# Keys in eight tiles, an account of the vector engine in the planner, and a reordered prologue

## Chip, core and metric

The kernel runs on one core of one Trainium2 chip. The metric is the device time of one execution in microseconds (us); a kernel's time is the median of its runs.

## What is computed

Two independent halves over 2048 positions of width 512, written side by side. Half A is attention with 32 query heads of width 16 that share one head of keys and values. Half B is a short and a long causal convolution per channel, with a multiplicative gate before and behind the long one.

```python
def _A_ref(x, wq, wk, wv, wo):
    q = (x @ wq).reshape(B, S, H, Dh).transpose(0, 2, 1, 3)
    k = x @ wk
    v = x @ wv
    scores = jnp.einsum("bhqd,bkd->bhqk", q, k) * (Dh ** -0.5)
    p = _softmax(scores, axis=-1)
    o = jnp.einsum("bhqk,bkd->bhqd", p, v)
    return o.transpose(0, 2, 1, 3).reshape(B, S, H * Dh) @ wo

def _B_ref(q, k, v, shift_k, ssm_k, ssm_D):
    k_shift = sum of four shifted copies of k times shift_k
    kv = k_shift * v
    y = irfft(rfft(pad(kv)) * rfft(pad(ssm_k)))[:S] + kv * ssm_D
    return q * y

return jnp.concatenate([a, b], axis=-1)
```

## The kernel before

**Engines.** TensorE (PE) does the products, ScalarE (ACT) the exponentials of the softmax, VectorE (DVE) reads the products out of PSUM and does the arithmetic of half B, GpSimd (POOL) some casts and many DMA issues, SyncE (SP) the other DMAs. Each engine runs its queue in order. The order on each is the order in which the program emits instructions (`manual_schedule`).

**Attention.** The scores are computed transposed: keys on the partitions, 512 queries of two head halves on the free axis. The work is cut into 32 stacks (`NQ`), each of 16 tiles of 128 keys times two halves `a`; with a few of them taken out (below) that makes 1016 score tiles, numbered u in the code. For each u, `scores` (through `keys`, L1039) issues eight matmuls of `kst` (keys, f16, with rows for the low parts and for a bound) against `st` (queries of the stack) into one of two PSUM buffers of the pool `ps`; `exp` (L1056) makes `p` out of it on ACT; `pv` (L1080) multiplies `p` with `vx` (values and a row of ones) and accumulates in a pair of PSUM banks `acc`, from the pool `pf`, over a whole stack. At a stack's end DVE adds the two banks into `ao` (L1089, L1090) and a DMA sends it to `od`. The softmax's shift is a bound from norms, not the true maximum; a row of `st` carries it.

**The filler.** `pf` has two pairs. One is held by the accumulation of the stack, the other goes in turn to all other products: query projections, the Fourier products of half B (`halves`, L250), the output projection. These are Python generators ("threads"): `own`, `wo_heads`, `conv_pe`, `conv_short`, `rest_of_q`, `wo_part`, `conv_dve`, `spill`. A thread yields `(n, cost, NEW or CONT, ...)` for n units of products, `(0, cost)` for DVE work, or `(WAIT, x)` to be asked again 2x score slots later. After each score tile `_Fill.turn` gives a slot's spare PE time (`SLOT` = 916 ns less `SCORES` = 220 and `PV` = 430 for each accumulation) to the first thread that fits, and DVE work against a credit of `RATE` = 850 ns for each slot. A thread that is in the middle of its products holds the pair (`holder`, CONT); after its last product the next NEW one is let in `GAP` = 2 slots later. The planner does not know how far behind DVE is. `after(...)` lets a thread wait until another has emitted something.

**The early stretch.** The prologue transposes x, projects the first queries, finds the maximum of the absolute keys (`kv_max`, L630), from which `k_max` and `k_row` (L649 to L653) make a clipped maximum over all keys and `wbn` (L831) the row of bounds. `k_first` (L624) makes the first 512 keys, `k_cut` and `k_split` (L664, L671, L673) clip them and split them into `kst`. Two products with `sel` place the queries (L823, L827), one with `wbn` (L833) adds the bound, and `st` is copied from PSUM. The other three chunks of 512 keys are made in `rest_of_q` among the first 32 score tiles (`k_chunk`, `v_turn`), out of the tile `kvt`.

**`own`.** In the stacks `OWN_IN` (27 to 30) the last key tile is not exponentiated by ACT: `own` puts its scores into the fill pair (a = 0, then a = 1), DVE reads each twice (L1137, L1138) and computes the exponential as a polynomial (L1148), and the result is accumulated by `pv` when `attend` finds it in `owed`.

## Time and profile before

| what | us |
|---|---|
| median of 3 runs | 1009.33 |
| the three runs | 1011.52, 1009.33, 1003.33 |
| the profiled execution, whole | 1009.57 |
| its span, first to last instruction | 1007.7 |

The profile is of one execution. Its rows give the start and the busy time of groups of instructions, an engine and a line of the kernel, and what is written from what. A bracket `[0.98 <-POOL wkv L273]` gives the engine's idle time ahead of the group and the instruction that ended it. A row `x14` stands for 14 instructions that overlap or follow closely. Page 5's groups end in the busy time, the mean duration in ns, and the idle time just before. In the windows, each engine has its busy time and its number of instructions, then come the clock that PE was granted (1.00 is full), the share of the DMA engines and GB/s. The mean granted clock of the execution was 0.988.

### The profile page before, as it was taken

Reading aid. Unit: us, or ns where it says so; the run is one execution under the profiler, and the core shown is the slowest. Engines: PE = TensorE matmul, PEld = TensorE weight load, DVE = VectorE, ACT = ScalarE, POOL = GpSimd, SP = SyncE. Lnnn points to the kernel's source line nnn. Section 1 sums busy time; section 2 is a strip of 40 time slices with the busy share of each in tenths; the row PEclk is TensorE's granted clock in tenths of the full one; section 3 lists DMA queues with packets and bytes.
Section 4 is the critical chain, followed back from the end, with each engine's and each line's share of the span. In section 5 each row is a group of like instructions: output and inputs, shape, how many; then the busy total and the mean of one; then the engine's idle time right before and its main releaser. Section 6 shows DMA issues by size and latency. Waiting matters only on the chain.

```text
span 1007.7 us, 51389 instructions
## 1 busy us (share of the span) xinstructions
PE 945.7 (94%) x23517; PEld 460.7 (46%) x23517; DVE 751.1 (75%) x985; ACT 952.5 (95%) x1031; POOL 173.2 (17%) x320
## 2 busy tenths in 40 slices
PE   7899989989999999999999999999989999989996
PEld 4334544435454444444444445544434444444453
DVE  4555578789529989989898568789979947576853
ACT  4779999999999999999999999999999999999994
POOL 6031122321113000101433332000000122200000
PEclk9979999999999999999999999999999999999999
DMA  7242343332114212321343333110121232221101
GB/s 246 96 119 69 96 136 106 86 98 65 53 42 135 62 42 74 109 63 54 110 124 122 115 96 94 43 53 31 59 85 44 74 124 88 76 64 32 33 25 47
DMA packets 69207, 82.94 MB, mean 82 GB/s; under 512 B 20753, under 2 KB 58295, under 8 KB 68983
## 3 DMA queue, kind: packets, MB, share of 16 engines
q1 hardware_dynamic: 47558, 43.48, 13.6%
q0 software_dynamic: 20320, 35.46, 12.0%
q8 instruction: 186, 3.05, 1.3%
q10 hardware_dynamic: 1104, 0.64, 0.2%
q14 instruction: 39, 0.31, 0.1%
HBM read 54.46 MB, written 25.03 MB: 79 GB/s over the span
## 4 chain that ended last, share of the span: by engine, by line
PE 49%; ACT 30%; DVE 12%; issue 7%; POOL 1%; DMA 1%; ACTq 0%; DVEq 0%
ACT p L1056 30%; PE f L1080 24%; PE s L1039 14%; PE f L250 10%; DVE own L1148 2%; DVE sp L169 2%; DVE ao L1089 1%; DVE ao L1090 1%; DMA wkvf<-in_A_wk 1%; DVE sp L290 1%; DVE sp L435 0%; PE f L638 0%; DVE sp L219 0%; PE f L658 0%; DVE u L218 0%
## 5 line engine op out<-in xcount | busy, mean ns | idle before, releaser
L1056 ACT ACTIVATE p<-s 128x1024 f32<-128x1024 f32 x1012 | 935.7, 1068 | 28.9 <-PE s L1039 26.7
L1080 PE MATMUL f<-p,vx 64*32 64x512 f32 (+1 forms) x8848 | 551.0, 558 | 2.9 <-DVE sp L290 2.1
L1039 PE MATMUL s<-st,kst 49*32 49x512 f16 x8128 | 425.8, 383 | 34.6 <-ACT p L1056 26.9
L1039 PEld LDWEIGHTS <-kst 49*32 49x32 f16 x8192 | 197.5, 90 | 402.1 <-issue 350.5
L1080 PEld LDWEIGHTS f<-p,vx 64*32 64x32 f32 x8848 | 175.4, 107 | 32.6 <-issue 6.2
L169 DVE TENSOR_TENSOR sp<-sp 128x1024 f32<-128x1024 f32 x96 | 111.0, 1214 | 0.0
L290 DVE COPY sp<-f 128x1024 f32<-128x1024 f32 x32 | 39.1, 1223 | 68.0 <-PE f L250 68.0
L295 POOL DMA_DIRECT2D ff<-in_ff x64 | 35.2, 556 | 266.3 <-ACT p L1056 265.4
L250 PE MATMUL f<-wo,o 64*32 64x512 f16 x1440 | 56.9, 375 | 1.9 <-DVE r L468 1.6
L169 DVE TENSOR_TENSOR sp<-sp,sp 128x1024 f32<-128x1024 f32 x48 | 56.3, 1217 | 0.3
L250 PE MATMUL f<-xT,wq 64*32 64x512 f16 x1344 | 51.9, 375 | 0.0
L1089 DVE COPY ao<-f 128x512 f32<-128x512 f32 (+1 forms) x33 | 22.2, 674 | 36.8 <-PE f L1080 36.7
L295 POOL DMA_DIRECT2D fi<-in_fi x32 | 17.4, 547 | 181.2 <-ACT p L1056 180.4
L250 PE MATMUL f<-a,ff 64*32 64x256 f32 x1024 | 42.3, 382 | 3.4 <-DVE t L396 1.5
L250 PE MATMUL f<-sp,fi 64*32 64x256 f32 x1024 | 40.5, 376 | 2.0 <-DVE r L468 2.0
L250 PE MATMUL f<-hT,ff 64*32 64x256 f32 x1024 | 40.7, 377 | 0.7 <-DVE sp L290 0.4
L470 POOL DMA_DIRECT2D out<-r x32 | 17.3, 546 | 128.1 <-DVE r L468 128.1
L468 DVE TENSOR_TENSOR r<-f,q 128x512 f32<-128x512 f32 x16 | 11.0, 690 | 31.9 <-PE f L250 31.8
L405 DVE TENSOR_TENSOR a<-a,t 128x512 f32<-128x512 f32 x48 | 33.2, 691 | 1.5
L396 DVE TENSOR_TENSOR t<-kk,tpb 128x512 f32<-128x512 f32 (+1 forms) x50 | 33.0, 663 | 0.0
L323 POOL DMA_DIRECT2D hin<-in_B_ssm_k x32 | 21.1, 663 | 58.6 <-ACT p L1056 57.1
L250 PEld LDWEIGHTS <-o 64*32 64x32 f16 x1440 | 22.4, 93 | 17.0 <-issue 3.2
(191 smaller groups left out, 747.3 us busy)
## 6 DMA issues: line engine op xcount, KB each, us to landing
ff<-in_ff POOLq DMA_DIRECT2D x64, 128.0 KB, 2.6
od<-ao SPq DMA_DIRECT2D x60, 128.0 KB
qd<-qp SPq DMA_DIRECT2D x48, 128.0 KB
st<-qd SPq DMA_DIRECT2D x62, 98.0 KB
kk<-in_B_k POOLq DMA_DIRECT2D x32, 128.0 KB, 2.4
v<-in_B_v POOLq DMA_DIRECT2D x32, 128.0 KB, 3.0
hin<-in_B_ssm_k POOLq DMA_DIRECT2D x32, 128.0 KB, 5.8
fi<-in_fi POOLq DMA_DIRECT2D x32, 128.0 KB, 3.3
```

What stands on the lines that cost most here:

```text
L169: v.tensor_tensor(part(out), part(a), part(b), op)
L250: y = self.nc.tensor.matmul(out[j : j + 32, cols], w[r, j : j + 32], x[r], start=half == m == 0, stop=half == 1 and m == k - 1,)
L290: self.nc.vector.tensor_copy(out, self.both.rearrange("p i (q n) -> p i q n", q=2))
L295: self.paced(self.nc.gpsimd.dma_start(t[:, i], self.I[n][:, 2 * m2 + i]))
L323: self.paced(nc.gpsimd.dma_start(dst, src))
L396: nc.vector.tensor_tensor(out[:, n], kk[:, x], tap(i, n.stop - n.start), ALU.mult)
L405: nc.vector.tensor_tensor(a, a, t, ALU.add)
L1039: self.nc.tensor.matmul(s[j : j + 32, e, :], self.kst[rows, k * P + j : k * P + j + 32], self.st[n][rows, a, cols], start=True, stop=True,)
L1056: self.exps[u % 4] = self.nc.scalar.activation(self.pt[u], s, AF.Exp, scale=LN2 * DH**-0.5 / SC / SC)
L1080: nc.tensor.matmul(self.acc[e][32 * j : 32 * j + 32, m], vx[rows, :], y, start=k == 0, stop=stop)
L1089: nc.vector.tensor_copy(a, self.acc[0][:, m])
L1148: v.scalar_tensor_tensor(g, g if i < 4 else y, c[i], y if i else x.bitcast(BF16), ALU.add, ALU.mult)
```

## The change

**Account of DVE.** The emitter keeps `now` (the score slot), `dve` (the planner's time at which DVE will have done all that has been given to it) and `ready` (such times for the pairs, one appended whenever a holder gives up a pair or an accumulation ends, one removed whenever a pair is taken). `charge` adds a cost, `due` asks if a time has come, `mark` records when a named result will be there.

```diff
     def pair(self):
+        del self.ready[:1]
         return self.pf.tile([P, 2, 512], F32, tag="f", name=self.nm("f"))
+    def charge(self, cost, pe):
+        self.dve = max(self.dve, SLOT * self.now + 700 * pe) + cost
+    def due(self, t):
+        return SLOT * self.now + 300 >= t
+    def mark(self, x):
+        self.seen.add(x)
+        self.when[x] = self.dve
     def after(self, *what):
-        while not self.seen.issuperset(what):
-            yield WAIT, 1
+        while not all(x in self.seen and self.due(self.when.get(x, 0)) for x in what):
+            yield WAIT, 0.5
...
-                    if n < 1 or self.holder not in (None, t) or (self.holder is None and i < self.free):
+                    if n < 1 or self.holder not in (None, t):
+                        continue
+                    if self.holder is None and (i < self.free or not self.em.due(self.em.ready[0])):
                         continue
...
-                self.credit -= a[1] if n == a[0] else 0
+                if n == a[0]:
+                    self.credit -= a[1]
+                    self.em.charge(a[1], n > 0)
```

So a NEW product is let in only when the next pair is counted as free. In `own`, the wait between the two halves' keys changes, and in `attend` the owed accumulation waits for its account:

```diff
                 if a == 0:
-                    yield WAIT, 1.5, CONT
+                    self.ready.append(self.dve)
+                    yield WAIT, 1, CONT
+                    while not self.due(self.ready[0]):
+                        yield WAIT, 0.5, CONT
...
-            if self.owed and self.owed[0][0] == -1 - n:
+            self.now = x
+            if self.owed and self.owed[0][0] == -1 - n and self.due(self.owed_at):
```

**Keys in tiles.** `kst` becomes eight tiles of 256 keys, `kvt` two tiles of 256; the maximum for the values' guard is taken in two pieces, and the transposes of the last 32 rows of values come one wait later.

```diff
-        self.kst = self.c.tile([P, S], F16, name="kst")
+        self.kst = [self.c.tile([P, CB], F16, name=f"kst{i}") for i in range(S // CB)]
...
-                    self.kst[rows, k * P + j : k * P + j + 32],
+                    self.kst[k // 2][rows, k % 2 * P + j : k % 2 * P + j + 32],
...
-        self.kvt = self.w.tile([P, 512], F32, tag="of", bufs=1, name="kv")
-        v.tensor_copy(self.kvt[0:96], kvb[0:96, 0, :])
+        self.kvt = [self.w.tile([P, CB], F32, tag=x, bufs=1, name="kv") for x in ("of", "r")]
+        for h in range(2):
+            v.tensor_copy(self.kvt[h][0:96], kvb[0:96, 0, CB * h : CB * h + CB])
...
+        yield WAIT, 0.5, CONT
         yield 1, 300, CONT, 1
         self.v_turn(r, kvb[:, 0, :])
-        yield WAIT, 0.5, CONT
```

**Prologue.** POOL makes `sel` and `wb`, splits the key columns of `wkv` and only then fills `wkx`; the split of the value columns comes after `k_first`. All sixteen `kv_max` come before `k_first`. The queries are placed last, and ACT copies both halves of `st`:

```diff
         self.kv_max(kh, range(3), (2, 3))
-        self.k_first(kb, 0, range(4))
         self.kv_max(kh, (3,), (2, 3))
-        self.k_first(kb, 0, range(4, 12))
+        self.k_first(kb, 0, range(8))
+        self.kv_parts(slice(DH, 32))
...
+        self.k_split(0, self.k_cut(kb[:, 0, 0:CB]), 0)
+        nc.scalar.copy(self.xa[:, 2:4], t3[1])
         for a in both:
-            nc.tensor.matmul(b[:, a, :], self.wbn[:, a, :], qa, start=False, stop=True)
-        self.k_split(0, kc, 0)
-        nc.scalar.copy(self.xa[:, 2:4], t3[1])
-        nc.vector.tensor_copy(st[:, 0, :], b[:, 0, :])
-        nc.scalar.copy(st[:, 1, :], b[:, 1, :])
-        self.k_first(kb, 1, range(8))
+            b = (self.wide if a else self.pair)()[:, 0, :]
+            for i in both:
+                nc.tensor.matmul(b, self.sel[:, a, i, :], qp[:, i, :], start=i == 0, stop=False)
+            nc.tensor.matmul(b, self.wbn[:, a, :], qa, start=False, stop=True)
+            nc.scalar.copy(st[:, a, :], b)
         self.exp(0, self.scores(0))
-        self.k_first(kb, 1, range(8, 12))
+        self.k_first(kb, 1, range(6))
         self.exp(1, self.scores(1))
+        self.k_first(kb, 1, range(6, 12))
```

Lines shift: what is L1039 before is L1055 in the changed file, L1056 is L1072, L1080 is L1096, L250 is L264, L1137 and L1138 are L1153 and L1154.

On DVE at the end of the prologue, before (`x` is the buffer of the maximum, `ks` the scalars made of it, `kc`, `kh` and `kst` the first keys, `st` the queries):

```order
L815 TENSOR_REDUCE ks<-x_266 128x1
L649 TENSOR_SCALAR ks<-msk,ks 128x4
L664 TENSOR_SCALAR kc_307<-f_267,msk 128x256
L653 TENSOR_REDUCE ks<-x_266 128x1
L831 TENSOR_SCALAR wbn<-msk,ks 128x4
L671 CAST kh_315<-kc_307 128x256
L673 SCALAR_TENSOR_TENSOR kst<-kh_315,msk,kc_307 128x256
L836 CAST st_301<-f_302 128x512
L664 TENSOR_SCALAR kc_354<-f_267,msk 128x256
```

And after:

```order
L829 TENSOR_REDUCE ks_300<-x_19_271 128x1
L665 TENSOR_SCALAR ks_300<-msk_81,ks_300 128x4
L669 TENSOR_REDUCE ks_300<-x_19_271 128x1
L840 TENSOR_SCALAR wbn_139<-msk_81,ks_300 128x4
L680 TENSOR_SCALAR kc_23_314<-f_20_272,msk_81 128x256
L687 CAST kh_24_316<-kc_23_314 128x256
L689 SCALAR_TENSOR_TENSOR kst0_112<-kh_24_316,msk_81,kc_23_314 128x256
L680 TENSOR_SCALAR kc_29_363<-f_20_272,msk_81 128x256
```

The clipping `kc` moves behind `wbn`, and the copy of `st` is gone from DVE.

On PE in stack 27, the first matmul of each piece from the 850th score tile on, before (`s` are scores, `f_2212` the accumulation of the stack, `f_2248` and `f_2257` the keys of `own` for a = 0 and a = 1):

```order
L1039 MATMUL s_2246_19256<-st_2129_18264,kst_115 32x512
...
L1039 MATMUL f_2248_19267<-st_2213_19002,kst_115 32x512
...
L1039 MATMUL s_2249_19278<-st_2129_18264,kst_115 32x512
...
L1080 MATMUL f_2212_18993<-p_2239_19215,vx_116 32x512 x2
...
L1039 MATMUL s_2251_19298<-st_2129_18264,kst_115 32x512
...
L1039 MATMUL s_2253_19309<-st_2129_18264,kst_115 32x512
...
L1080 MATMUL f_2212_18993<-p_2247_19265,vx_116 32x512 x2
...
L1039 MATMUL s_2255_19328<-st_2129_18264,kst_115 32x512
...
L1039 MATMUL f_2257_19339<-st_2213_19002,kst_115 32x512
```

After (`f_2249` and `f_2254` are the keys of `own`):

```order
L1055 MATMUL s_2247_19270<-st_2130_18278,kst4_116 32x512
...
L1055 MATMUL f_2249_19281<-st_2214_19016,kst7_119 32x512
...
L1055 MATMUL s_2250_19292<-st_2130_18278,kst4_116 32x512
...
L1096 MATMUL f_2213_19007<-p_2240_19229,vx_120 32x512 x2
...
L1055 MATMUL s_2252_19312<-st_2130_18278,kst5_117 32x512
...
L1055 MATMUL f_2254_19323<-st_2214_19016,kst7_119 32x512
```

Between the two sets of keys stood the scores of four slots, and now those of two.

On PE from the 100th score tile on, before (`f_304` is a Fourier product of `a`, the gated input of half B; `f_308` the accumulation):

```order
L1039 MATMUL s_301_2518<-st_216_1894,kst_115 32x512
...
L250 MATMUL f_304_2532<-a_257_2200,ff_253_2173 32x256
...
L1039 MATMUL s_306_2544<-st_216_1894,kst_115 32x512
...
L1080 MATMUL f_308_2555<-p_290_2455,vx_116 32x512 x2
...
L1039 MATMUL s_310_2568<-st_216_1894,kst_115 32x512
```

After, from the same score tile and then from the 105th on (`f_321` is the product of `a`, `f_307` the accumulation):

```order
L1055 MATMUL s_302_2533<-st_217_1908,kst1_113 32x512
...
L1055 MATMUL s_305_2546<-st_217_1908,kst1_113 32x512
...
L1096 MATMUL f_307_2557<-p_291_2470,vx_120 32x512
...
L1055 MATMUL s_317_2637<-st_217_1908,kst2_114 32x512
...
L1055 MATMUL s_319_2657<-st_217_1908,kst2_114 32x512
...
L264 MATMUL f_321_2668<-a_256_2195,ff_254_2187 32x256
```

The product of `a` comes six score tiles later.

More of the change, by code (lines that the diff above doesn't have):

```diff
@@ L120, in __init__ @@
         self.step = self.slot = 0
-        self.seen = set()
+        self.seen, self.when = set(), {}
+        self.now = self.dve = 0
+        self.ready = []
     def nm(self, s):
@@ L657, in k_chunk @@
         r, a = slice(32 * c, 32 * c + 32), CB * h
-        self.nc.tensor.matmul(b[:, a : a + CB], self.msk[r, 163:291], self.kvt[r, a : a + CB], start=True, stop=True)
+        self.nc.tensor.matmul(b[:, a : a + CB], self.msk[r, 163:291], self.kvt[h][r, :], start=True, stop=True)
         self.k_split(c, self.k_cut(b[:, a : a + CB]), h)
@@ L820, in prologue @@
         self.st[0] = st
-        b = self.pair()
-        for i in both:
-            nc.tensor.matmul(b[:, 0, :], self.sel[:, 0, i, :], qp[:, i, :], start=i == 0, stop=False)
         self.k_max(kh[:, 0:4], km)
-        kc = self.k_cut(kb[:, 0, 0:CB])
-        for i in both:
-            nc.tensor.matmul(b[:, 1, :], self.sel[:, 1, i, :], qp[:, i, :], start=i == 0, stop=False)
+        self.k_first(kb, 0, range(8, 12))
         self.k_row(kmr, kh[:, 0:4])
@@ L919, in rest_of_q @@
         self.k_chunk(2, kvb[:, 1, :], 1)
-        v.tensor_copy(self.kvt[r], kvb[r, 0, :])
+        for h in range(2):
+            v.tensor_copy(self.kvt[h][r], kvb[r, 0, CB * h : CB * h + CB])
         yield WAIT, 1, CONT
@@ L1184, in attend @@
                 self.pv(*y)
+                if y[2:] == (True,):
+                    self.charge(1400, True)
+                    self.ready.append(self.dve)
                 if y[2:] == (True,) and n in OWN_IN:
@@ L1385, in give @@
                 self.free = i + gap
+                self.em.ready.append(self.em.dve)
     def turn(self, i, pvs, more):
```

43 lines of the change are left out of this document (24 added, 19 removed).

## Prediction

> **What bounds the kernel now.** I read the page first: busy shares, the chain that ended last, the largest group.
>
> ```profile
> span 1007.7 us, 51389 instructions
> ...
> PE 945.7 (94%) x23517; PEld 460.7 (46%) x23517; DVE 751.1 (75%) x985; ACT 952.5 (95%) x1031; POOL 173.2 (17%) x320
> ...
> PE 49%; ACT 30%; DVE 12%; issue 7%; POOL 1%; DMA 1%; ACTq 0%; DVEq 0%
> ...
> L1056 ACT ACTIVATE p<-s 128x1024 f32<-128x1024 f32 x1012 | 935.7, 1068 | 28.9 <-PE s L1039 26.7
> ```
>
> ACT and PE are both near 95%. ACT does one thing from the first exponential to the last: 1016 of them. Where it runs undisturbed, the timeline of ACT gives their rate, and the end points of that chain:
>
> ```profile
> 25.55 3.90 ACT L1056 ACTIVATE pfirst<-s 128x1024 f32<-128x1024 f32 x4
> ...
> 260.39 176.32 ACT L1056 ACTIVATE p<-s 128x1024 f32<-128x1024 f32 x191 [0.23 <-PE s L1039]
> ...
> 977.46 16.61 ACT L1056 ACTIVATE p<-s 128x1024 f32<-128x1024 f32 x18 [0.28 <-PE s L1039]
> ```
>
> 176.32 us for 191 exponentials is 0.92 us each, so 1016 need about 938 us. The first starts at 25.55, the last ends at 994.07, which is 968.5 us: the other 30 us are idle time of ACT, and the group's row says the same (28.9, of which 26.7 behind the scores of PE). So the span of 1007.7 us is a prologue of 25.55, the exponentials 938, stalls of ACT about 30, and a tail of 13.6. The exponentials themselves and the tail are not touched by the change. It can act in two places: the prologue, and the stalls. PE runs its queue in order, so a product or an accumulation that waits for DVE to empty a pair of PSUM banks holds up the scores behind it, and when that is longer than the two score buffers cover, ACT stalls.
>
> **Prologue.** The path to the first exponential runs through the maximum over the keys. The rows of the timeline up to the row of bounds `wbn`:
>
> ```profile
> 18.16 1.02 ACT L606 ACTIVATE xT<-x 128x1024 f16<-128x1024 f32 x1
> ...
> 19.10 1.04 PE L630 MATMUL x<-xT,wkv 128*32 128x512 f16 x14 [0.98 <-POOL wkv L273]
> ...
> 20.61 0.60 PE L630 MATMUL x<-xT,wkv 128*32 128x512 f16 x2
> ...
> 21.26 0.69 DVE L815 TENSOR_REDUCE ks<-x 128x1 f32<-128x512 f32 x1 [2.08 <-PE x L630]
> ...
> 23.05 0.23 DVE L831 TENSOR_SCALAR wbn<-msk,ks 128x4 bf16<-128x4 f32 x1
> ```
>
> The first fourteen of the matmuls for the maximum wait 0.98 for POOL's split of `wkv`, and the last two come after four of `k_first`. After the change POOL makes that split before `wkx` is filled, and no `k_first` stands between. Then the last input is ACT's cast, done at 18.16 + 1.02 = 19.18; two matmuls of 0.60 in all and two handovers of 0.05 (20.61 + 0.60 = 21.21 to 21.26) let the reduction start at 19.88 instead of 21.26, 1.38 earlier. The chain behind it, 21.26 to 23.05 + 0.23 = 23.28, is the same instructions, so `wbn` is ready at 21.90.
>
> From `wbn` to the first score:
>
> ```profile
> 22.24 0.54 DVE L664 TENSOR_SCALAR kc<-f,msk 128x256 f32<-128x256 f32 x1
> ...
> 23.19 0.71 DVE L671 CAST kh<-kc 128x256 f16<-128x256 f32 x1
> ...
> 23.35 0.61 PE L833 MATMUL f<-qa,wbn 128*128 128x512 bf16 x2
> ...
> 23.93 0.48 DVE L673 SCALAR_TENSOR_TENSOR kst<-kh,msk,kc 128x256 f16<-128x256 f16 x1
> 24.34 0.68 DVE L836 CAST st<-f 128x512 f16<-128x512 f32 x1
> ...
> 25.05 0.59 ACT L837 CAST st<-f 128x512 f16<-128x512 f32 x1 [3.54 <-DVE st L836]
> 25.07 0.41 PE L1039 MATMUL s<-st,kst 49*32 49x512 f16 x8 [0.25 <-DVE st L836]
> ...
> 26.64 0.29 DVE L671 CAST kh<-kc 128x256 f16<-128x256 f32 x1
> ```
>
> Before, DVE does `kh`, `kst` and a half of `st` one after the other, and the score waits for the last. Now DVE has `kc` behind `wbn`, then `kh` and `kst`: 21.90 + 0.54 + 0.71 + 0.48 = 23.63 and about 0.1 between them. Beside it ACT copies both halves of `st`: the products with `wbn` begin about 21.96 and take 0.61 for both halves in the row above, with the query products of the second half now between them; from about 22.6 two copies of 0.59 end near 23.8. Both arms meet at 23.75 to 23.8, so the first score starts near 23.8 instead of 25.07 and the term is **−1.3 us**. Bounds: the second query product needs a score buffer that ACT's copy of `t3` has to free, and if the two copies each wait for PE another 0.9 goes (−0.4); if `kh` takes 0.29 as in the row at 26.64 and ACT keeps up, −1.8. The `k_first` half that moves behind the first two scores keeps PE busy when only four exponentials are ahead; it is as many matmuls as before. POOL's casts of the v columns come later, but are needed only by `rest_of_q`. That work is hidden; without the cover it would cost its own 0.4.
>
> **Keys in eight tiles, transposes a slot later.** The early stretch has most of the idle time. A row of the windows by engine, and two of ACT's stalls in it:
>
> ```profile
> 25.50:66.00 40.50, 35.01 (x521) 12.40 (x529) 20.86 (x43) 28.21 (x30) 8.12 (x15) 0.83 0.38 114
> ...
> 45.81 4.05 ACT L1056 ACTIVATE p<-s 128x1024 f32<-128x1024 f32 x4 [1.76 <-PE s L1039]
> ...
> 59.01 1.02 ACT L1056 ACTIVATE p<-s 128x1024 f32<-128x1024 f32 x1 [1.89 <-PE s L1039]
> ```
>
> ACT is busy 28.21 of 40.50 us, so 12.3 us of the 30 lie here. One tile `kst` could make a score wait for a chunk that it doesn't read. But the stalls come where a score needs the chunk that has just been made (every fourth score from the 16th on), and in the changed program the same scores still wait for the same DVE instruction. I take **0**. Bounds: +0.5 (four more small DVE instructions and the copy of `kvt` in two), and −3.7 if both stalls shown, 1.76 + 1.89, were false waits.
>
> **The account of DVE.** Comparing the two programs, the first matmul of the following late work no longer stands ahead of the DVE instruction that it waited for; ACT's stalls there, exactly as ACT's timeline has them:
>
> ```profile
> 135.63 1.03 ACT L1056 ACTIVATE p<-s 128x1024 f32<-128x1024 f32 x1 [1.29 <-PE s L1039]
> 137.63 58.92 ACT L1056 ACTIVATE p<-s 128x1024 f32<-128x1024 f32 x64 [0.98 <-PE s L1039]
> ...
> 437.81 41.41 ACT L1056 ACTIVATE p<-s 128x1024 f32<-128x1024 f32 x45 [1.10 <-PE s L1039]
> ...
> 577.62 135.30 ACT L1056 ACTIVATE p<-s 128x1024 f32<-128x1024 f32 x146 [1.65 <-PE s L1039]
> ...
> 890.76 27.82 ACT L1056 ACTIVATE p<-s 128x1024 f32<-128x1024 f32 x30 [1.58 <-PE s L1039]
> 919.91 35.11 ACT L1056 ACTIVATE p<-s 128x1024 f32<-128x1024 f32 x38 [1.32 <-PE s L1039]
> 955.83 21.35 ACT L1056 ACTIVATE p<-s 128x1024 f32<-128x1024 f32 x23 [0.82 <-PE s L1039]
> ```
>
> The product that read `a` at the 100th score now stands at the 106th; the one at 437 us is moved; at 577 from the 570th to the 572nd; at 890 and 919 the pair is taken later; the own-tile accumulation at 955 goes two slots earlier, with its DVE chain ahead of it. Sum 1.29 + 0.98 + 1.10 + 1.65 + 1.58 + 1.32 + 0.82 = **−8.74**. The other stalls sit where the order has not changed.
>
> It also makes waits. `own` now queues the second half's keys two score slots behind the first, where it was four, in each of the four stacks. Rows of the first of these in before, and of one accumulation that waited for a copy:
>
> ```profile
> 836.73 1.23 DVE L1137 TENSOR_SCALAR own<-f 128x1024 f32<-128x1024 f32 x1 [0.87 <-PE f L1039]
> ...
> 837.87 0.41 PE L1039 MATMUL s<-st,kst 49*32 49x512 f16 x8
> 837.99 1.22 DVE L1138 SCALAR_TENSOR_TENSOR own<-own,f 128x1024 f32<-128x1024 f32 x1
> 838.63 0.41 PE L1039 MATMUL s<-st,kst 49*32 49x512 f16 x8 [0.35 <-ACT p L1056]
> ...
> 435.12 1.22 DVE L290 COPY sp<-f 128x1024 f32<-128x1024 f32 x1
> ...
> 436.39 1.09 PE L1080 MATMUL f<-p,vx 64*32 64x512 f32 x16 [1.05 <-DVE sp L290]
> ...
> L169 DVE TENSOR_TENSOR sp<-sp 128x1024 f32<-128x1024 f32 x96 | 111.0, 1214 | 0.0
> ```
>
> The pair is free when DVE has read it twice, at 837.99 + 1.22 = 839.21. Two slots behind, PE reaches the keys about 0.2 after the score at 837.87, near 838.1: it waits 1.1. The row at 436.39 shows what such an idle PE costs ACT: 1.05 of PE became a stall of 1.10 (437.81). A little is covered here, because PE was 0.35 ahead of ACT at the next score; I take 0.9 each, 4 × 0.9 = +3.6. Behind the waiting keys stand the next scores, and behind those the accumulation of the stack. Two more places get a new wait: an accumulation near the 325th score whose pair is freed by a DVE instruction that now stands behind one L169 of 1.214 us (+1.0, between 0 and 1.2), and a product near the 428th behind one copy L290 of 1.22 (+0.65, between 0 and 1.2). Sum +3.6 + 1.0 + 0.65 = **+5.25**.
>
> **The clock.** Some stalls drag a stretch of half clock after them. Windows of 3.40 us, PE's busy time first and its granted clock ahead of the last two columns:
>
> ```profile
> 130.40:133.80 3.40, 1.71 (x40) 0.51 (x24) 2.54 (x4) 3.40 (x5) 2.84 (x6) 1.00 0.53 152
> 133.80:137.20 3.40, 3.21 (x48) 1.42 (x53) 3.33 (x7) 1.56 (x2) 0.35 (x1) 0.50 0.82 244
> ...
> 886.90:890.30 3.40, 1.60 (x48) 0.60 (x37) 3.37 (x4) 2.28 (x3) 0.29 (x1) 1.00 0.10 34
> ```
>
> PE half busy (1.71 of 3.40) was followed by a window at 0.50; 1.60 of 3.40 elsewhere was at full clock, so where the gap lies in the clock's own grid counts. A new wait of 1.1 between busy stretches leaves 2.3 of 3.40 busy, so I charge no clock to it. If one of them does fall badly, a window at half rate loses up to 1.7 us of PE time: four give +6.8, the upper end.
>
> The Trainium skill's page "TensorE: Matmul & The Clock Gate" (Part 1, the HAM clock gate) says that the rate is halved after at least one idle window of about 3.4 us. The trace disagrees: the window ahead of the drop had 1.71 us of work in it. By the page the new waits could never cost clock and this upper end falls away; the forecast is the same.
>
> **The sum.** 1009.57 − 1.3 + 0 − 8.74 + 5.25 = 1004.8. The profiled execution took 1009.57 (1.9 outside its span), 0.24 above the median of the three runs, so I keep 1004.8 and say 1004.5 for the median. The three runs of before spread over 8 us, so a change of 1%, about 10 us (below 999.2, above 1019.4), is what a measurement can tell from none.
>
> **Rivals.**
> - *The account works and makes no new waits* (DVE is quicker at those six places than I think). 1009.57 − 1.3 − 8.74 = 999.5. For it: DVE is only 75% busy. Against it: at the four keys the two rows of 1.23 and 1.22 leave no room in two slots of 0.92. Chance 0.18; it lies on the boundary of 1%, half to each side.
> - *The tiles remove false waits* in the early stretch. 1004.8 − 3.7, and the half-clock windows that follow go too (of the 12.3 us idle perhaps 4 more): 997. Against it: the same waits in the order. Chance 0.08.
> - *Stalls move and are not removed*, so it becomes slower: a product put later meets DVE behind another chain, since DVE is loaded three quarters and every product ends in a read of 0.7 to 2.4 us. Then the −8.74 goes and the +5.25 stays: 1009.57 − 1.3 + 5.25 = 1013.5, and 1020 with the four half-clock windows. It decides when more than 1.3 + 8.74 − 5.25 = 4.8 us of new stalls appear elsewhere. For it: the account lets a waiting product poll twice as often and counts DVE's costs with the planner's rough prices. Against it: the waits that I could follow in the order are gone. Chance 0.20, a quarter of that over 1019.4.
> - *The half-clock windows of the early stretch fall otherwise*, since everything starts 1.3 us earlier in a grid that isn't the kernel's: ±4 us on 1004.8, as the runs of before show. Chance 0.14, to 1000.8 or 1008.8.
>
> **Numbers.** My own forecast, 1004.5 with 1001 to 1008.5, has the remaining 0.40. Faster by over 1%: 0.09 + 0.08 + 0.04 of the forecast's and the clock's lower edges = 0.21. Slower: 0.05 + 0.04 for a cause that none of these names = 0.09. Same: 0.70. The range leaves out one tenth at each end: 997 to 1014.
>
> **What would show it.** First exponential near 24.3, not 25.55; the reduction for the maximum near 19.9. In the early stretch ACT's idle time stays near 12 us, and scores still wait for `kst`. No stall of ACT at the scores 101, 422, 571, 907, 937 and 975. New PE waits of about 1.1 on DVE's second read, four of them, from the 850th score on. ACT's idle time in all falls from 28.9 to about 25. I am wrong if ACT's idle time doesn't fall, if the keys' waits are absent or longer than 2 us, or if new waits for DVE stand at places that this list doesn't have.

## The result and the profile after

| | before | after |
|---|---|---|
| median of 20 runs, us | 1010.75 | 1003.96 |
| lowest and highest | 1003.02, 1015.23 | 999.47, 1008.06 |
| profiled execution: whole, span | 1009.57, 1007.7 | 1002.79, 1001.0 |
| first exponential starts, last ends | 25.55, 994.07 | 24.39, 987.95 |
| mean granted clock | 0.988 | 0.991 |

The ratio is 0.995, with a 95% interval of 0.9932 to 0.9969: the kernel is a little faster, by half a per cent. The forecast was 1004.5. Below, medians and ratios are of fast executions: one execution each of "keys four slots apart", "changed, again" and "the early chunks spread" was slow (1880, 1034 and 1752 us) and is left out.

The page of the changed kernel, the same places as before (L1072 is the exponential, L1096 the accumulation, L1055 the scores):

```profile
span 1001.0 us, 51398 instructions
...
PE 942.8 (94%) x23517; PEld 459.5 (46%) x23517; DVE 750.0 (75%) x988; ACT 953.2 (95%) x1032; POOL 172.7 (17%) x321
...
PE 56%; ACT 27%; DVE 11%; issue 5%; ACTq 0%; DVEq 0%
...
L1072 ACT ACTIVATE p<-s 128x1024 f32<-128x1024 f32 x1012 | 935.5, 1069 | 23.5 <-PE s L1055 21.7
```

The exponentials' busy time is what it was (935.7, now 935.5). Their idle time fell from 28.9 to 23.5. Where it fell is read from ACT's timeline, behind the early stretch. A group in it ends where ACT next stalls, so each bracket is one stall, and adding up the counts gives the score at which it stands (counted from 0, like u in the code; the first row begins at the 27th):

```profile
64.95 55.88 ACT L1072 ACTIVATE p<-s 128x1024 f32<-128x1024 f32 x60 [1.11 <-PE s L1055]
121.28 72.90 ACT L1072 ACTIVATE p<-s 128x1024 f32<-128x1024 f32 x79 [0.44 <-PE s L1055]
195.22 58.93 ACT L1072 ACTIVATE p<-s 128x1024 f32<-128x1024 f32 x64 [1.04 <-PE s L1055]
255.24 88.34 ACT L1072 ACTIVATE p<-s 128x1024 f32<-128x1024 f32 x96 [1.09 <-PE s L1055]
344.74 50.75 ACT L1072 ACTIVATE p<-s 128x1024 f32<-128x1024 f32 x55 [1.16 <-PE s L1055]
395.75 44.59 ACT L1072 ACTIVATE p<-s 128x1024 f32<-128x1024 f32 x48 [0.26 <-PE s L1055]
440.82 35.15 ACT L1072 ACTIVATE p<-s 128x1024 f32<-128x1024 f32 x38 [0.48 <-PE s L1055]
...
835.15 33.43 ACT L1072 ACTIVATE p<-s 128x1024 f32<-128x1024 f32 x36 [0.81 <-PE s L1055]
869.11 27.77 ACT L1072 ACTIVATE p<-s 128x1024 f32<-128x1024 f32 x30 [0.53 <-PE s L1055]
897.41 27.77 ACT L1072 ACTIVATE p<-s 128x1024 f32<-128x1024 f32 x30 [0.53 <-PE s L1055]
925.71 45.35 ACT L1072 ACTIVATE p<-s 128x1024 f32<-128x1024 f32 x49 [0.53 <-PE s L1055]
```

The seven stalls that were to go (135 to 138, 437, 577, 890, 919 and 955 us in the profile before) are gone. New ones stand at the scores 326 (1.16), 381 (0.26) and 429 (0.48, where 1.10 stood at the 422nd), and four at the 853rd, 889th, 919th and 949th (0.81 and three times 0.53), each one just behind the second half's keys of `own`. The wait behind those four, on PE, with DVE's two reads of the first keys ahead of it (columns as before; L1153 and L1154 are the two reads):

```profile
831.58 1.23 DVE L1153 TENSOR_SCALAR own<-f 128x1024 f32<-128x1024 f32 x1 [0.88 <-PE f L1055]
...
832.71 0.41 PE L1055 MATMUL s<-st,kst 49*32 49x512 f16 x8
832.84 1.22 DVE L1154 SCALAR_TENSOR_TENSOR own<-own,f 128x1024 f32<-128x1024 f32 x1
834.11 0.41 PE L1055 MATMUL f<-st,kst 49*32 49x512 f16 x8 [0.99 <-DVE own L1154]
```

832.84 + 1.22 = 834.06, and the keys start at 834.11, 0.99 after PE was free.

In the prologue, the same chain as before, maximum to first score:

```profile
18.34 1.67 PE L646 MATMUL x<-xT,wkv 128*32 128x512 f16 x16
...
20.05 0.69 DVE L829 TENSOR_REDUCE ks<-x 128x1 f32<-128x512 f32 x1 [0.73 <-PE x L646]
...
22.59 0.44 DVE L687 CAST kh<-kc 128x256 f16<-128x256 f32 x1
...
23.07 0.79 DVE L689 SCALAR_TENSOR_TENSOR kst<-kh,msk,kc 128x256 f16<-128x256 f16 x1
23.24 0.58 ACT L848 CAST st<-x 128x512 f16<-128x512 f32 x1
23.91 0.41 PE L1055 MATMUL s<-st,kst 49*32 49x512 f16 x8 [0.71 <-DVE kst L689]
```

The sixteen matmuls for the maximum run without a break, the reduction starts at 20.05 instead of 21.26, and the first score waits for `kst`, with the copy of `st` done just before it (23.82).

### The profile page after: what moved, and what is told of

Read it like the earlier page. It is cut to its first block, busy times and chain, and to the rows that moved or that the text cites. A ratio compares the mean times of both kernels' runs of the same rounds, so it can differ in the third digit from the quotient of the medians.

```text
span 1001.0 us, 51398 instructions
## 1 busy us (share of the span) xinstructions
PE 942.8 (94%) x23517; PEld 459.5 (46%) x23517; DVE 750.0 (75%) x988; ACT 953.2 (95%) x1032; POOL 172.7 (17%) x321
## 4 chain that ended last, share of the span: by engine, by line
PE 56%; ACT 27%; DVE 11%; issue 5%; ACTq 0%; DVEq 0%
ACT p L1072 26%; PE f L1096 26%; PE s L1055 16%; PE f L264 11%; DVE sp L183 2%; DVE own L1153 1%; DVE own L1154 1%; DVE ao L1105 1%; DVE sp L304 1%; DVE ao L1106 1%; DVE own L1167 0%; DVE sp L449 0%; DVE t L449 0%; PE f L610 0%; DVE wp L1281 0%
## 5 line engine op out<-in xcount | busy, mean ns | idle before, releaser
L1072 ACT ACTIVATE p<-s 128x1024 f32<-128x1024 f32 x1012 | 935.5, 1069 | 23.5 <-PE s L1055 21.7
L1096 PE MATMUL f<-p,vx 64*32 64x512 f32 (+1 forms) x8848 | 547.5, 556 | 3.4 <-DVE wp L1281 1.1
L1055 PE MATMUL s<-st,kst 49*32 49x512 f16 x8128 | 422.9, 382 | 34.1 <-ACT p L1072 24.3
L1055 PEld LDWEIGHTS <-kst 49*32 49x32 f16 x8192 | 196.6, 90 | 407.7 <-issue 349.5
L1096 PEld LDWEIGHTS f<-p,vx 64*32 64x32 f32 x8848 | 173.6, 106 | 30.9 <-issue 3.9
L264 PE MATMUL f<-wo,o 64*32 64x512 f16 x1440 | 56.8, 375 | 0.4 <-DVE wp L1281 0.2
L264 PE MATMUL f<-xT,wq 64*32 64x512 f16 x1344 | 51.7, 375 | 0.5 <-DVE gm L750 0.5
L264 PE MATMUL f<-a,ff 64*32 64x256 f32 x1024 | 41.6, 378 | 0.7 <-PE s L1055 0.6
L264 PE MATMUL f<-hT,ff 64*32 64x256 f32 x1024 | 40.7, 377 | 1.5 <-DVE sp L304 1.3
L264 PE MATMUL f<-sp,fi 64*32 64x256 f32 x1024 | 40.1, 376 | 0.3 <-DVE r L482 0.3
L482 DVE TENSOR_TENSOR r<-f,q 128x512 f32<-128x512 f32 x16 | 11.0, 690 | 32.6 <-PE f L264 32.6
L1167 DVE SCALAR_TENSOR_TENSOR own<-own,own 128x1024 f32<-128x1024 f32 x24 | 29.4, 1224 | 0.7
```

Of the source, the lines that this page charges most:

```text
L264: y = self.nc.tensor.matmul(out[j : j + 32, cols], w[r, j : j + 32], x[r], start=half == m == 0, stop=half == 1 and m == k - 1,)
L1055: self.nc.tensor.matmul(s[j : j + 32, e, :], self.kst[k // 2][rows, k % 2 * P + j : k % 2 * P + j + 32], self.st[n][rows, a, cols], start= ...
L1072: self.exps[u % 4] = self.nc.scalar.activation(self.pt[u], s, AF.Exp, scale=LN2 * DH**-0.5 / SC / SC)
L1096: nc.tensor.matmul(self.acc[e][32 * j : 32 * j + 32, m], vx[rows, :], y, start=k == 0, stop=stop)
L1167: v.scalar_tensor_tensor(g, g if i < 4 else y, c[i], y if i else x.bitcast(BF16), ALU.add, ALU.mult)
```

## The experiments

Each kernel was timed in five rounds beside the kernel before on the same chip; ratios are to that. The first four rows were timed on one chip, the next four on a second, then two on a third and two on a fourth; across these groups only the ratios compare.

| run | median, us | ratio, 95% interval |
|---|---|---|
| new prologue alone | 1007.94 | 0.9991 (0.9962 to 1.0019) |
| tiles alone | 1012.06 | 1.0034 (1.0012 to 1.0056) |
| account alone | 1002.79 | 0.9945 (0.9914 to 0.9976) |
| changed, keys four slots apart | 1008.54 | 0.9986 (0.9958 to 1.0013) |
| changed, again | 1003.98 | 0.9947 (0.9919 to 0.9974) |
| changed, without the tiles | 1004.31 | 0.9950 (0.9922 to 0.9978) |
| changed, transposes in the old place | 1002.57 | 0.9954 (0.9927 to 0.9981) |
| changed, keys three slots apart | 1003.65 | 0.9942 (0.9915 to 0.9970) |
| changed, chunks of keys early | 996.11 | 0.9875 (0.9834 to 0.9916) |
| ... and keys three slots apart | 993.63 | 0.9859 (0.9818 to 0.9901) |
| ... and the early chunks spread | 992.98 | 0.9850 (0.9818 to 0.9882) |
| ... the same without the tiles | 993.81 | 0.9852 (0.9822 to 0.9881) |

The intervals are some 0.6% wide, about 6 us, so a step of 1 us is judged by the stalls in the profiles. Most of these repeat to within 0.05 us in every kernel that has them (0.56 at the 550th score, 1.12 at the 717th); those at the 166th and 230th do not, and no step rests on them.

### The three parts alone

The prologue alone: the change's edits of `load`, `places`, `prologue`, nothing else.

```diff
-        self.k_first(kb, 0, range(4))
         self.kv_max(kh, (3,), (2, 3))
-        self.k_first(kb, 0, range(4, 12))
+        self.k_first(kb, 0, range(8))
+        self.kv_parts(slice(DH, 32))
```

> The kernel before with the new prologue alone. Theory: the maximum starts about 1.2 us earlier and the first exponential at 24.3 to 24.5 instead of 25.55; nothing behind it takes the gain back, so the time falls by 1.2 us (ratio 0.9988), give or take where the half-clock windows fall. ACT's stalls behind 66 us stay as before (1.29 and 0.98 near 135, 1.10 near 437, 1.65 near 577, 1.58, 1.32, 0.82 at the end). Rival: the early stretch is bound by the keys' chunks and takes the 1.2 us back; then it ends at 65.7 as before and the ratio is 1.000.

Its first exponential starts at 24.50, 1.05 earlier than in before. Behind it, ACT's stalls are those of before, but for one stretch: near 577 us the old stall of 1.65 had half clock behind it in this execution and became 1.93 and 1.11. So the span of its profile is 1008.1, while the early gain is there. A stall is new, 0.29 at the score numbered 3, and it is in every profile with the new prologue: with six products of `k_first` behind each of the first two scores, score 3 starts on PE 3.5 us behind the first, where it was 2.9. The early stretch ended at 65.39, where before had 65.67, so in this execution most of the 1.05 was gone again by then. The interval of the ratio holds both 0.9988 and 1.000. So the earlier start is shown: 24.19 to 24.79 in the eleven profiles with the new prologue, 25.55 to 26.19 in the three with the old one. A net gain of time is not shown.

The tiles alone: `kst` in eight, `kvt` in two, the maximum in two pieces, the transposes one wait later.

```diff
-        self.kst = self.c.tile([P, S], F16, name="kst")
+        self.kst = [self.c.tile([P, CB], F16, name=f"kst{i}") for i in range(S // CB)]
...
+        yield WAIT, 0.5, CONT
         yield 1, 300, CONT, 1
         self.v_turn(r, kvb[:, 0, :])
-        yield WAIT, 0.5, CONT
```

> The kernel before with the eight tiles of keys, the two tiles of kvt and the later transposes alone. Theory: the waits on kst are true ones, so ACT's stalls of 1.76, 1.82 and 1.89 in the early stretch stay and the ratio is 1.000 to 1.0005. Rival: the waits were false ones; two of them go, 3.7 us less, ratio 0.996.

The rival falls: the stalls before the scores 16 and 20 are 1.76 and 1.80, as in before, so these were true waits. But the kernel is slower, which neither expected. Three lines of ACT's timeline of this run, for the scores 24 to 26, where before had 1.89, 0.48 and 0.71:

```profile
60.48 1.02 ACT L1060 ACTIVATE p<-s 128x1024 f32<-128x1024 f32 x1 [2.52 <-PE s L1043]
62.15 1.02 ACT L1060 ACTIVATE p<-s 128x1024 f32<-128x1024 f32 x1 [0.65 <-PE s L1043]
64.83 1.02 ACT L1060 ACTIVATE p<-s 128x1024 f32<-128x1024 f32 x1 [1.65 <-PE s L1043]
```

The 1.65 stands in the changed kernel too, and a later run takes it apart. In this profile the first exponential also starts 0.64 later than in before (26.19); 0.52 of it stands already at ACT's last cast of x (18.68), ahead of everything that the edit touches.

The account alone: the change's edits of `_Fill`, `attend`, `own`, `after` and the marks.

> The kernel before with the account of DVE alone. Theory: the change's gain behind 66 us is all here: seven stalls with 8.74 us in all go, four waits for the second half's keys come (0.5 to 0.8 us of ACT each, 2.4 in all), one near the 325th score (1.2) and one near the 428th (0.5). Sum -4.6 us, ratio 0.9955. Rival: the stalls only move, and the account is worth less than 2 us (ratio above 0.998).

```diff
-                    if n < 1 or self.holder not in (None, t) or (self.holder is None and i < self.free):
+                    if n < 1 or self.holder not in (None, t):
+                        continue
+                    if self.holder is None and (i < self.free or not self.em.due(self.em.ready[0])):
                         continue
```

The theory holds. ACT's stalls behind the 30th score sum to 9.20 us, in before to 15.12, in the changed kernel to 9.22, and they stand at the same scores as in the changed kernel. The account is the gain; prologue and tiles add nothing to it that the times show.

### The keys of `own`: two, three and four slots apart

> The changed kernel, but the second half's keys of own come four score slots behind the first, as in before, instead of two. Theory: the four waits of PE for DVE's second read (about 1.0 us each) and ACT's four stalls behind them (0.81 and three of 0.53, 2.4 us in all) go, and nothing takes their place: 1001.6 us, ratio to the kernel before 0.9925 where the changed kernel has 0.995. Rival: the fill pair is held two slots longer, later products come later and wait elsewhere; then the stalls stay 21 to 22 us in all and the time 1004.

```diff
-                    yield WAIT, 1, CONT
+                    yield WAIT, 1.5, CONT
```

The rival holds, by more than it said: the ratio is 0.9986, where the changed kernel has 0.995. The two intervals overlap by 0.001, and the stalls decide: behind the 30th score ACT's are 13.83 us, where the changed kernel has 9.22. The end of ACT's timeline of this run:

```profile
891.53 1.02 ACT L1072 ACTIVATE p<-s 128x1024 f32<-128x1024 f32 x1 [2.19 <-PE s L1055]
893.67 26.69 ACT L1072 ACTIVATE p<-s 128x1024 f32<-128x1024 f32 x29 [1.11 <-PE s L1055]
921.68 46.16 ACT L1072 ACTIVATE p<-s 128x1024 f32<-128x1024 f32 x50 [1.32 <-PE s L1055]
969.57 6.54 ACT L1072 ACTIVATE p<-s 128x1024 f32<-128x1024 f32 x7 [1.73 <-PE s L1055]
```

The four small stalls of the keys are gone, and two of the large ones of before are back at the same scores: 2.19 and 1.11 at the 907th, with half clock behind it in this execution, and 1.32 at the 937th (before 1.58 and 1.32). The third, 0.82 at the 975th, is not back; the 1.73 stands at the 987th and is a new one. At the 907th, PE waits for a read by DVE (L482) that has only begun behind the polynomial of `own` (L1167); at the 987th it waits for DVE's `o`, which waits for a DMA:

```profile
888.06 1.22 DVE L1167 SCALAR_TENSOR_TENSOR own<-own,own 128x1024 f32<-128x1024 f32 x1
889.20 0.68 DVE L482 TENSOR_TENSOR r<-f,q 128x512 f32<-128x512 f32 x1
889.94 1.07 PE L264 MATMUL f<-sp,fi 64*32 64x256 f32 x16 [1.80 <-DVE r L482]
...
966.40 0.69 DVE L1239 TENSOR_TENSOR o<-of,r 128x512 f16<-128x512 f32 x1 [8.20 <-DMA r<-rd]
...
968.59 0.62 PE L264 MATMUL f<-wo,o 64*32 64x512 f16 x16 [1.04 <-DVE o L1239]
```

The same read of L482 and the product behind it in the changed kernel:

```profile
879.33 0.69 DVE L482 TENSOR_TENSOR r<-f,q 128x512 f32<-128x512 f32 x1
...
882.64 0.63 PE L264 MATMUL f<-sp,fi 64*32 64x256 f32 x16
```

With the keys two slots earlier the read is done long before PE comes to the product, although the product stands two scores earlier too: that much of the cause is read from these rows; that the spacing sets it is shown by the run. So the account's wait in `own` costs 2.4 us and saves the 2.9 of before at the 907th and 937th and, in this kernel, the one at the 987th.

> The changed kernel with the second half's keys of own three score slots behind the first, behind that slot's accumulation. The pair is then free before PE arrives (DVE's second read ends 2.5 us behind the first keys, three slots are 2.76), so PE doesn't wait; the queue of that slot is 0.2 us too long, so ACT's four stalls fall from 2.4 in all to 0.8, and the time by 1.6 to about 1002.4. Rival, from the run with four slots: later products meet the pair one slot later and wait; then stalls of over 1 us stand near the 907th, 937th or 987th score and the time is 1005 or more.

```diff
-                    yield WAIT, 1, CONT
+                    yield WAIT, 1.5, CONT
...
-                    n = min(a[0], room) // a[3] * a[3]
+                    n = a[0] if t is self.threads[0] and self.holder is t else min(a[0], room) // a[3] * a[3]
```

Each is right in part. The four stalls at the keys are gone, PE doesn't wait there, and no large stall is back. But three of 0.59, 0.59 and 0.54 stand instead (scores 867, 897 and 927): 1.7 us in place of 2.4, a gain of 0.7 where 1.6 was expected. They are the rival's kind of wait, only smaller and at other scores; the row of PE ahead of the first:

```profile
844.50 0.67 PE L264 MATMUL f<-sp,fi 64*32 64x256 f32 x16 [0.81 <-DVE r L482]
```

The median is 0.3 below the changed kernel's beside it, which is less than the runs can tell.

### Chance, tiles and transposes

> The changed kernel once more, beside the others on the same chip. 1003 to 1005 us. ACT's stalls behind the first 30 scores at the same places as in its first profile (9.2 us in all); only stretches of half clock may lie elsewhere.

The stalls stand at the same scores, 9.45 us in all against 9.22. Two differ: the one of 1.04 at the 166th is absent, and the one at the 230th has grown. There is the same accumulation, waiting for the same copy by DVE for 1.04 and 1.05, in the first profile of the changed kernel and in the second; behind it ACT's stall:

```profile
253.82 1.09 PE L1096 MATMUL f<-p,vx 64*32 64x512 f32 x16 [1.04 <-DVE sp L304]
...
255.24 3.77 ACT L1072 ACTIVATE p<-s 128x1024 f32<-128x1024 f32 x4 [1.09 <-PE s L1055]
```

```profile
252.80 1.96 PE L1096 MATMUL f<-p,vx 64*32 64x512 f32 x16 [1.05 <-DVE sp L304]
...
255.29 1.02 ACT L1072 ACTIVATE p<-s 128x1024 f32<-128x1024 f32 x1 [2.17 <-PE s L1055]
```

Sixteen matmuls take 1.09 in one and 1.96 in the other: in the second, PE had half its clock. So a gap of 1.05 in PE's work costs ACT 1.09 or 2.17 plus 0.21, from one execution to the next; the last section has what decides. Over the twenty runs of the changed kernel the time goes with the mean granted clock, from 999.47 us at 0.995 to 1008.06 at 0.986. The difference of 0.009 is 9 us of a span of 1000, as large as the spread of the times. That such half-clock stretches make the spread is argued from these numbers; no run tests it.

> The changed kernel without the tiles: one kst, one kvt, the maximum in one piece and the transposes in their old place; account and prologue stay. If the tiles cost time, as the run of tiles alone says (ratio 1.0034), this is 2 to 4 us faster than the changed kernel: 1000 to 1002. If that run was chance of the clock's grid, it is the changed kernel's time within 1 us.

The last sentence of it holds: 1004.31 beside 1003.98. The edit is the change without its hunks on `kst`, `kvt` and `v_turn`.

> The changed kernel with its tiles, but the last transposes of values one slot earlier, where they were in before. If what the tiles cost comes from that step, the stall at the 26th score falls from 1.65 to 0.7 and the time by 1 to 3 us, as in the run without the tiles. If it comes from the split copies and the small instructions, the time stays at the changed kernel's.

```diff
-        yield WAIT, 0.5, CONT
         yield 1, 300, CONT, 1
         self.v_turn(r, kvb[:, 0, :])
+        yield WAIT, 0.5, CONT
```

In this run the stall at the 26th score is 0.70:

```profile
61.17 1.02 ACT L1072 ACTIVATE p<-s 128x1024 f32<-128x1024 f32 x1 [0.70 <-PE s L1055]
```

So the later transposes cost 0.95 us: they stand in one slot with the last chunk, which waits for DVE to read them out of the same bank. In the changed kernel (L696 the transposes, L674 the chunk):

```profile
59.96 0.63 PE L696 MATMUL f<-ident,kv 32*128 32x32 f32 x4
...
60.91 1.22 PE L674 MATMUL f<-kv,msk 32*128 32x256 f32 x2 [0.32 <-DVE vx L699]
```

The two together are the 0.95. The median is 1.4 below the changed kernel's. That explains about 1 of the 3.4 us of the tiles alone; the rest lies within that run's interval (from 1.2 us on) and is put down to no step.

### The early stretch

Of the changed kernel's 22.3 us of stalls, 13.1 lie before the 30th score, where the change gained nothing. This sum varies with the clock: in four profiles with the same early program it is 11.2 to 17.7. If they are the time from the making of a chunk to the score that reads it, making it earlier removes them:

> The changed kernel, but in the score slots 8 to 26 the planner may give four units of products more, so that each chunk of keys is made four slots ahead of the score that reads it, not one. Theory: the early stalls are waits for a chunk that has just been made, whatever the number of tiles; those before the scores 16, 20 and 24 (1.76, 1.81, 1.58) go, PE has as much work as before, and with less idle time of PE some stretches of half clock (1.7 us each) go too: the idle time of ACT in the first 30 scores falls from 13.1 to 6 to 8, and the time to 996 to 1000 (ratio 0.988 to 0.991). Rival: the early stretch is bound by PE's work; then the stalls move to the scores 10 to 15 and the time stays 1004.

```diff
+        room += 4 * (8 <= i < 27)
         more = True
         while more:
```

The theory holds: 996.11. Two lines of ACT's timeline of the changed kernel, at the scores 16 and 20, and two of this run at the scores 12 and 20:

```profile
45.38 4.05 ACT L1072 ACTIVATE p<-s 128x1024 f32<-128x1024 f32 x4 [1.76 <-PE s L1055]
51.24 1.02 ACT L1072 ACTIVATE p<-s 128x1024 f32<-128x1024 f32 x1 [1.81 <-PE s L1055]
```

```profile
38.96 1.02 ACT L1072 ACTIVATE p<-s 128x1024 f32<-128x1024 f32 x1 [0.70 <-PE s L1055]
...
51.70 1.02 ACT L1072 ACTIVATE p<-s 128x1024 f32<-128x1024 f32 x1 [2.03 <-PE s L1055]
```

The stall at the 16th score is 0.26 and that at the 24th is gone. Smaller ones came at the 12th and 13th (0.70 and 0.50) and at the 18th and 19th (0.55 and 1.04). The one at the 20th is not gone as expected: it is 2.03 and has another cause, since two chunks and the transposes are now made back to back there and PE waits for DVE between them (0.30 and 0.55), with half clock from 49.7 us on. Early stalls fall to 8.8 us, by less than expected, but below all of the four profiles above. Behind the 30th score, too, 2.5 us go (9.22 to 6.72); that was not expected, and the order there was not followed up. The edit gives more room to whatever product is next and not to the chunks alone; the chunks' part is read from the stalls at the 16th and 24th.

> The same with the second half's keys of own three slots behind the first. If both act by themselves: 0.7 to 1.0 us less than the run with the early chunks alone, with three or four stalls of 0.6 in place of 0.81 and three of 0.53 behind the 850th score. If the early chunks move the later products, new stalls behind score 30 take it back.

The edits are those of the two runs. 5.78 us of late stalls against 6.72: 0.9 less, as expected, of which the keys' stalls are 0.7; the median fell by 2.5.

> As the run with early chunks and keys three slots behind, but the four units more are given in the slots 8 to 16 only, so that the last two chunks and the transposes are not made back to back (there, PE waited for DVE between them, and ACT 2.03 before the 20th score). Theory: the stalls at the scores 19 to 21 (4.2 us in all) fall to under 2, half clock behind them goes: 990 to 992. Rival: the work is only moved, the stall comes at the 24th or 28th score, and the time stays 993 to 994.

```diff
-        room += 4 * (8 <= i < 27)
+        room += 4 * (8 <= i < 17)
```

The stall of 2.03 is gone, and half clock behind it. One of 0.94 at the 26th score came instead, and 1.75 us at the scores 9 to 11, where this execution had half clock and the other had not: the early stalls are 7.0 (8.8). By the times nothing is decided: 992.98 lies between the theory's 992 and the rival's 993, and the ratio moved by 0.0009, far less than its interval. By the profile it is half the theory's outcome (its span is 990.5 against 991.7). The windows from 25.5 to 66 us, of the changed kernel and of this one (PE, PEld, DVE, ACT and POOL with instructions, the granted clock third from the end):

```profile
25.50:66.00 40.50, 34.44 (x515) 12.30 (x514) 21.25 (x47) 27.01 (x28) 10.97 (x20) 0.83 0.40 118
```

```profile
25.50:66.00 40.50, 36.78 (x645) 13.82 (x643) 22.51 (x52) 32.96 (x34) 6.47 (x12) 0.96 0.27 86
```

In the same 40.5 us ACT does 6 us more, and PE's clock is 0.96 instead of 0.83.

> The same with one kst and one kvt (no tiles). With chunks made four slots ahead, a false wait would now show: a score that reads an old chunk would wait for DVE's writing of a new one, some 1 us each. If waits are kept by what is read, as the order says, the early stalls and the time are those of the run with tiles within 1 us.

As expected for the time: 993.81 beside 992.98. The early stalls are 8.2 against 7.0; the 1.2 more stand at the scores 9 to 11 (2.95 and 1.75), where this execution had more half clock. The tiles are worth nothing that these runs can tell, with early chunks as with late ones.

## Why the prediction was right, point by point

**Prologue**, forecast −1.3. Measured −1.16 from profile to profile and −1.05 in the run of this part alone. The reduction for the maximum started at 20.05, not 19.88, because ACT's last cast of x was 0.2 later in that execution (it starts at 18.34, not 18.16); from there to the first score it was 3.86 as forecast to within 0.1. `kh` took 0.44, not the 0.71 taken over, but `kst` 0.79, not 0.48. The same two take 0.29 and 0.48 a little later, when POOL has no cast running; beside POOL's casts they were longer by nearly the same sum in both kernels (0.42 and 0.46), at another place. Both arms met within 0.1, as worked out. What failed is the cover of `k_first`: behind the first two scores it was not hidden but cost 0.29 at score 3, in the first profile and in every later one with this prologue.

**Tiles**, forecast 0, bounds +0.5 and −3.7. The waits were true ones, as the two programs' order said. What was missed is the transposes' slot: +0.95, outside the upper bound. I had named it as part of the step and priced only the copies and the small instructions.

**The removed stalls**, forecast −8.74. All seven places are clear, so the size was right. The attribution was not: "at 890 and 919 the pair is taken later" is a reading of the order that the run with four slots refutes. In the changed kernel the product that waited at 890 stands two scores earlier, not later, and DVE's read is done before it. Those two (2.90 of the 8.74) went because `own` queues its keys nearer together, the very edit that the prediction, but for the place at 955, counted as a cost alone; with the keys four slots apart they come back. The one at 955 stays away in that run: there the own-tile accumulation comes later and finds DVE done (it starts at 957.22 and waits for nothing), which is what the account's wait in `attend` is for, while in the changed kernel it stands earlier, as predicted. So that one goes either way.

**The new waits**, forecast +5.25. The four key waits on PE were 0.99, forecast 1.1, and cost ACT 2.4, not 3.6: from 0.53 to 0.81 each instead of 0.9. I had taken nearly the whole wait over to ACT, and half to four fifths of it arrived. The 326th score cost 1.16 (forecast 1.0), the 429th 0.48 (0.65), and one of 0.26 at the 381st was not foreseen (PE waits 0.50 for DVE's L750). In all 4.3.

**What was not in the sum.** Late stalls fell by 5.9 (15.12 to 9.22): −8.74 + 4.30, and −1.46 at places where the order didn't change, of which 1.3 is one stall without half clock in this execution (1.09 at the 230th score, 2.17 and 0.23 before), with it in the second profile (2.17 and 0.21). The early stretch has 1.1 us more of stalls; 0.95 by the transposes and 0.29 by `k_first` would make it, but its sum also varies by several us with the clock. The tail was 0.6 shorter. These chances of the clock go both ways; the sum without them, −1.16 + 1.1 − 8.74 + 4.3 = −4.5, is near the forecast's −4.8. So the number was right because the largest term was, and because errors of about 1 us in smaller ones (tiles +0.95, keys −1.2) cancel. There is luck in it: the forecast started from 1009.57, and the median of before over twenty runs is 1010.75. The fall forecast was 4.8, the fall measured 6.8: a start that was 1.2 too low and a fall that was 2.0 too small nearly cancel. From profile to profile the fall is 6.8 too, and there the 2.0 are the 1.46 and the shorter tail.

**The signs.** First exponential 24.39 (24.3), four waits of 0.99 for DVE's second read (1.1), none of the six named stalls, ACT's idle time 23.5 (about 25). By its last sign the prediction was wrong in small things: waits for DVE at places that its list doesn't have stand at the 26th score (DVE's L699) and at the 381st.

**The rivals.** Moved stalls are real in this kernel: the run with four slots is that case, with a ratio of 0.9986. The clock's rival was bounded well: half-clock stretches moved, and no wait of 1.0 at the keys started one in any of the six profiles that have these waits. The Trainium skill's page "TensorE: Matmul & The Clock Gate" (Part 1, the HAM clock gate) has the grid run free of the kernel, and with that the traces agree: its place against the span's start differs from profile to profile (last section). With its condition of a whole idle window the trace doesn't agree: in the second profile PE was never idle for more than 1.05 us on the way into that stretch.

## What to carry to other kernels

When an engine runs its queue in order, ask of each stall not only what it waits for but what would have to be *queued earlier on the other engine* for the wait to be over: here the same two-slot move that made four waits of 1 us removed two larger stalls, and only undoing it alone showed that. A planner that ignores one engine's backlog is worth correcting even by rough prices, but the largest stalls may lie where it has no say: a larger budget in nineteen early slots, so that data are made four slots ahead of their reader, brought at least as much (ratio 0.9875 beside 0.9947) as the whole account (0.9945 beside 1). Where runs of one program spread by 8 us, read single steps from stalls in the trace, and let times decide only what is larger.

## What the runs showed of the hardware

The size of a gap doesn't say if PE loses its clock: gaps of 1.04 and 1.05 us at the same instruction of the same program ended with 1.09 us and 2.38 us of stall. In these traces the granted clock is 1.00 or 0.50, and up to the last exponential its stretches at 0.50 are 3.41, 6.83 or 10.24 us long, and the stretches at 1.00 between them are multiples of 3.41 too, so all changes lie on a grid of 3.41 us. Counted from the span's start, the grid lies 0.20 us behind a multiple of 3.41 in the first profile of the changed kernel, 0.18 in the second, and 2.60 in the run with four slots. Two windows of the grid in the second profile, and the two of the first profile that hold the same work:

```profile
249.36:252.77 3.41, 1.80 (x54) 0.67 (x39) 3.38 (x5) 3.41 (x5) 0.54 (x2) 1.00 0.55 163
252.77:256.18 3.41, 3.38 (x48) 1.56 (x56) 3.41 (x5) 1.24 (x2) 0.00 (x0) 0.50 0.16 57
```

```profile
249.38:252.80 3.42, 2.81 (x80) 1.24 (x64) 2.68 (x4) 3.42 (x5) 1.06 (x2) 1.00 0.37 114
252.80:256.21 3.41, 2.38 (x64) 1.22 (x65) 3.41 (x5) 2.32 (x4) 0.00 (x0) 1.00 0.33 106
```

In the second profile the gap of 1.05 and one of 0.51 ahead of it lie in one window, PE is busy for 1.80 us of it, and the next window is at half clock. In the first profile they lie in two, with 2.81 and 2.38 us busy, and the clock stays. The grid was in nearly the same place in both. What differed is that the work came 1.03 us later in the first, about as much as ACT's stall of 1.04 at the 166th score, which the second doesn't have.

Busy time in a window is not the whole rule: in the run of the prologue alone, a window of the grid with 1.60 us of work (from 887.70) was followed by full clock, and in the run of the tiles alone, one with 2.74 (from 32.71) by half clock. What else counts was not tested.

Where an early stretch has many gaps, as here, fewer gaps and more clock come together: 6.1 us of stalls went (13.1 to 7.0), and the stretch's clock rose from 0.83 to 0.96. Which part of the 6.1 is the clock's was not separated.
